# Loading and using the first two x tiles one after the other at the head of a fused state-space and feed-forward kernel

## The chip, the core and the metric

The kernel runs on one core of one Trainium2 chip. The metric is the device time of one launch in microseconds: 177.39 us before the change, the median of 3 runs (177.05 to 178.04).

## What is computed

The input x is 2048 tokens by 512 features. Both branches read its layer norm, and the output is their sum with x:

```python
x = A_x                                  # [1, 2048, 512]
xn = _layernorm(x, axis=-1)              # (x - mean) / sqrt(var + 1e-5)
# branch A: a diagonal complex state-space model, 512 states
Bu = einsum("bld,pd->blp", xn, B_bar)    # then h[t] = Lam_bar * h[t-1] + Bu[t]
y = 2.0 * einsum("blp,dp->bld", hseq, Cmat).real + xn * Dskip
# branch B: SwiGLU, w_gate and w_up [512, 1376], w_down [1376, 512]
z = (silu(xn @ w_gate) * (xn @ w_up)) @ w_down
return x + y + z
```

## The kernel before, in words

Tokens are cut into 16 tiles of 128 and four chunks of 512 (four tiles each). The 512 features are four blocks of 128 (`KD = 4`, index `k`; `HK = 2`). Most of the time is one long stream of matmuls on TensorE. In each chunk there are the projection to the states (L387), the gate and up projections (L462), the down projection (L630) and the state-space output (L643). VectorE does the rotations and scans of the state-space model beside them, and ScalarE (ACT) takes results out of PSUM.

Nothing reorders the instructions: each engine runs its own in the order in which the program emits them. From the second half of chunk 0 on, a backlog with a cost for each step (`queue`, `pump`, `need`) spreads VectorE's work between the matmuls. The head, with which the change deals, is written out by hand.

**Loads of the head (L128 to L146).** SP's queue loads x tile 0 (L128, 128 KB), then the four up rows (L133), then gate rows 0 and 1, x tile 2, gate row 2, x tile 3, gate row 3, the ends of both weights (`w_end`, L140 and L141) and x tiles 4 to 7 (L146). A row is one block `k` of 128 features by the first 1024 columns of a weight (256 KB, `load_row`, L122). Two groups of 512 columns are taken from it (`gi` 0 and 1). ACT's queue loads x tile 1 (L130), behind a small memset on VectorE (L129) that it has to wait for.

**Tiles 0 and 1 (L727 to L753).** Nine warming matmuls on constants run first (`dummy`, L703). Then the raw x tile is transposed on TensorE, block by block (`raw_mm`, L237). Meanwhile VectorE sums the rows of the tile (`sum_dve`, L229), and a small matmul subtracts the mean in PSUM (`cT_mean`, L245). Each block is then copied to SBUF by ACT (even `k`) or VectorE (odd `k`) (`raw_copy`, L252). The copies are the stationary operand of the up projection (`row_mm`, through `sw_mm`, L506). In `row_mm(0, k)`, row `k` of the up weights is multiplied for tile 0 and tile 1, with two column groups each: four matmuls of 512 columns, accumulated over `k` in four PSUM banks (`pair[0]`). The transposed blocks pass through the other four banks (`raw`): tile 0 has one bank for each block, and tile 1 has two banks with two blocks each.

**Around it.** VectorE computes the statistics of tiles 0 and 1 behind its copies (`ln_stats`, L189), GpSimd the reciprocal deviation `rstd` (L199), and VectorE the normalized tiles (`norm_dve`, L207). ACT scales the up results by `rstd` on the way out of PSUM (`sw_up`, L526). Gate row 0 follows on TensorE (`row_mm(1, 0)`), then the parameters' transpose (L278), gate rows 1 and 2, the transposes of the centered tile 2 (L237 again) and gate row 3. The normalized tiles are later transposed by SP's queue (L258), and the matrices B behind them (L150). TensorE reads those from about 23 us on (L387).

Of the kernel before, what the change touches and what calls it, by code (L numbers as in the profile page):

```python
# [23 lines left out]
def kernel(  # L24
# [17 lines left out]
    nc = tc.nc  # L42
# [9 lines left out]
    KD = D // 128  # L52
# [31 lines left out]
    x_v = A_x[0].rearrange("(n p) d -> p n d", p=128)  # L84
    out_v = out[0].rearrange("(n p) d -> p n d", p=128)
    wg_v = B_w_gate.rearrange("(k p) f -> p k f", p=128)
    wu_v = B_w_up.rearrange("(k p) f -> p k f", p=128)


    xall = const.tile([128, NT, D], BF16, name="xall")  # L90
# [5 lines left out]
    wu01 = const.tile([128, KD, FE], BF16, name="wu01")  # L96
# [24 lines left out]
    def load_row(q, t, view, k):  # L121
        q.dma_start(out=t[:, k, :], in_=view[:, k, 0:FE])  # L122

    HK = KD // 2
# [1 line left out]
    make_identity(nc, ident[:])  # L126
    minus_mean = const.tile([128, 128], BF16, name="minus_mean")
    nc.sync.dma_start(out=xall[:, 0, :], in_=x_v[:, 0, :])  # L128
    nc.vector.memset(xall[:, 1, 0:2], 0.0)  # L129
    nc.scalar.dma_start(out=xall[:, 1, :], in_=x_v[:, 1, :])  # L130
    nc.scalar.preload_act_table_set("silu_and_others")
    for k in range(KD):
        load_row(nc.sync, wu01, wu_v, k)  # L133
    for k in range(HK):
        load_row(nc.sync, wg01, wg_v, k)
# [49 lines left out]
    def by_k(ap):  # L185
        return ap.rearrange("p (k d) -> p k d", d=128)
# [36 lines left out]
    sums = const.tile([128, 2], BF16, name="sums")  # L223
# [4 lines left out]
    def sum_dve(i, dst):  # L228
        nc.vector.scalar_tensor_tensor(out=xnT[:, NCH - 1, i, 0:HW], in0=xall[:, i, 0:HW], scalar=1.0,  # L229
                                       in1=xall[:, i, HW:D], op0=ALU.mult, op1=ALU.add, accum_out=dst)  # L230
# [3 lines left out]
    raw = [pair[0][1] + pair[1][0], pair[1][1] * 2]  # L234

    def cT_mm(ps, src, k, first, stop):
        nc.tensor.matmul(ps[:, k * 128:(k + 1) * 128], lhsT=src[:, k * 128:(k + 1) * 128], rhs=ident[:], start=first,  # L237
                         stop=stop)

    def raw_mm(i):  # L240
        for k in range(KD):
            cT_mm(raw[i][k], xall[:, i, :], k, all(p is not raw[i][k] for p in raw[i][:k]), False)

    def cT_mean(i, *ks):
        nc.tensor.matmul(by_k(raw[i][ks[0]][:])[:, ks[0]:ks[-1] + 1:HK], lhsT=sums[:, i:i + 1].to_broadcast([128, 128]),  # L245
                         rhs=minus_mean[:, None, :].to_broadcast([128, len(ks), 128]), start=False, stop=True)

    def raw_copy(i, k):
        cT_copy(V.tensor_copy if k % 2 else nc.scalar.copy, raw[i][k], i, k, k + 1)

    def cT_copy(copy, ps, i, k0=0, k1=KD):
        copy(out=xcT[:, k0:k1, i * 128:(i + 1) * 128], in_=by_k(ps[:, k0 * 128:k1 * 128]))  # L252
# [21 lines left out]
    V = nc.vector  # L274
# [228 lines left out]
    def sw_mm(ps, groups, gi, i, k0=0, k1=KD):  # L503
        a, b = fgroups[gi]
        for k in range(k0, k1):
            nc.tensor.matmul(ps[:, 0:(b - a) * 128], lhsT=tokens(i, k), rhs=groups[gi][:, k, 0:(b - a) * 128],  # L506
                             start=(k == 0), stop=(k == KD - 1))
# [219 lines left out]
    dummy(warm, 4, CW)  # L727
    dummy(warm, 5, 128)
    nc.vector.tensor_scalar(out=minus_mean[:], in0=ident[:], scalar1=-1.0 / D, scalar2=None, op0=ALU.mult)
    for i in range(2):  # L730
        sum_dve(i, sums[:, i:i + 1])
    raw_mm(0)
    for k in range(HK):
        cT_mean(0, k)
        raw_copy(0, k)
    raw_mm(1)
    for k in range(HK, KD):
        cT_mean(0, k)
    for k in range(HK):
        cT_mean(1, k, k + HK)  # L740
        raw_copy(1, k)
    for k in range(HK, KD):
        raw_copy(0, k)
    for k in range(HK, KD):
        raw_copy(1, k)

    def row_mm(which, k):
        for i in range(2):
            for gi in range(2):
                sw_mm(pair[which][i][gi], (U, G)[which], gi, i, k, k + 1)  # L750

    for k in range(KD):
        row_mm(0, k)  # L753
    for i in range(2):
        ln_stats(i)
        ln_rstd(i, i + 1)
# [3 lines left out]
    for n in range(2):  # L760
        norm_dve(n)
    row_mm(1, 0)
    pp = prm_transpose()
    ln_stats(2)
# [6 lines left out]
    for k in range(1, SW):  # L771
        row_mm(1, k)
# [172 lines left out]
```

## Time and profile before

| | us |
|---|---|
| median of 3 runs | 177.39 (177.05 to 178.04) |
| the profiled execution | 178.12 |
| its span | 176.0 |
| busy: TensorE, weight loads, VectorE, ACT, GpSimd | 171.0, 82.0, 157.4, 102.3, 27.1 |
| x tile 0 arrives, by VectorE's first sum | 3.07 |
| first matmul with an up row | 4.82 |
| first matmul with up row 1 | 6.49 |
| first matmul with gate row 0 | 9.08 |

The span runs from the first to the last recorded instruction, and the time of the launch is 2.12 us longer. In the profile's rows a group of instructions stands with its line, engine, operation, `out<-in` and count; what is in brackets is the idle time of the engine ahead of it and what ended it. PE is TensorE, PEld its weight loads, DVE VectorE, POOL GpSimd, SPq and ACTq the sequencers of SP and ACT that issue DMAs. A matmul of 512 columns is recorded with some 379 ns from start to end, but matmuls overlap, so the distance between two starts is what one costs.

### The profile page before, as it was taken

Reading aid. Unit: us, or ns where it says so; the run is one execution under the profiler, and the core shown is the slowest. Engines: PE = TensorE matmul, PEld = TensorE weight load, DVE = VectorE, ACT = ScalarE, POOL = GpSimd, SP = SyncE. Lnnn points to the kernel's source line nnn. Section 1 sums busy time; section 2 is a strip of 40 time slices with the busy share of each in tenths; the row PEclk is TensorE's granted clock in tenths of the full one; section 3 lists DMA queues with packets and bytes.
Section 4 is the critical chain, followed back from the end, with each engine's and each line's share of the span. In section 5 each row is a group of like instructions: output and inputs, shape, how many; then the busy total and the mean of one; then the engine's idle time right before and its main releaser. Section 6 shows DMA issues by size and latency. Waiting matters only on the chain.

```text
span 176.0 us, 2435 instructions
## 1 busy us (share of the span) xinstructions
PE 171.0 (97%) x878; PEld 82.0 (47%) x894; DVE 157.4 (89%) x260; ACT 102.3 (58%) x188; POOL 27.1 (15%) x36
## 2 busy tenths in 40 slices
PE   8899999999999999999999999999999999999993
PEld 5444445564444464444444444446444444444542
DVE  3767999999999999999999999999999999589642
ACT  3179589794996689976044362014666652983100
POOL 5234110022000000000302500014100000530700
PEclk9999999999999999999999999999999999999999
DMA  5998969999999300220005830006310000597741
GB/s 152 370 342 80 194 110 181 303 202 293 169 207 274 115 4 0 50 61 0 2 4 111 94 34 0 0 4 68 53 22 0 0 4 0 70 164 124 93 89 60
DMA packets 34027, 18.05 MB, mean 103 GB/s; under 512 B 24512, under 2 KB 32832, under 8 KB 33888
## 3 DMA queue, kind: packets, MB, share of 16 engines
q1 hardware_dynamic: 30272, 14.39, 35.0%
q0 software_dynamic: 3456, 3.28, 14.6%
q10 hardware_dynamic: 288, 0.23, 0.4%
q8 instruction: 7, 0.11, 0.3%
q14 instruction: 4, 0.03, 0.1%
HBM read 8.33 MB, written 5.24 MB: 77 GB/s over the span
## 4 chain that ended last, share of the span: by engine, by line
PE 94%; DMA 3%; issue 1%; SPq 0%; ACT 0%; DVE 0%; ACTq 0%
PE ps L462 29%; PE ps L630 20%; PE ps L643 16%; PE ps L387 16%; PE ps L506 7%; PE ps L555 3%; DMA wu<-in_B_w_up_dram 3%; PE ps L805 2%; PE ps L620 2%; ACT u L489 0%; SPq L122 0%; SPq L128 0%; DVE xall L646 0%; PE ps L237 0%; PE ps L278 0%
## 5 line engine op out<-in xcount | busy, mean ns | idle before, releaser
L429 DVE TENSOR_TENSOR_SCAN g<-r_t,car,u 128x512 bf16<-128x512 f32 x24 | 28.8, 1263 | 0.0
L643 PE MATMUL ps<-CF,wt 128*128 128x512 bf16 (+2 forms) x133 | 28.2, 366 | 0.2
L387 PE MATMUL ps<-xnT,BT 128*128 128x512 bf16 x125 | 28.1, 379 | 0.2
L630 PE MATMUL ps<-wd_sb,guT 128*128 128x512 bf16 (+2 forms) x129 | 26.5, 362 | 0.1
L462 PE MATMUL ps<-xnT,wu 128*128 128x512 bf16 x94 | 24.5, 379 | 0.2
L462 PE MATMUL ps<-xnT,wg 128*128 128x512 bf16 x93 | 24.3, 379 | 0.1
L389 ACT CAST u<-ps 128x512 bf16<-128x512 f32 x32 | 17.8, 591 | 5.0 <-PE ps L387 4.1
L489 ACT CAST u<-ps 128x512 bf16<-128x512 f32 x30 | 17.8, 592 | 4.8 <-PE ps L462 4.8
L643 PEld LDWEIGHTS <-wt 128*128 128x128 bf16 x136 | 12.9, 98 | 15.0 <-DVE xall L600 0.4
L387 PEld LDWEIGHTS <-BT 128*128 128x128 bf16 x128 | 12.5, 98 | 14.9 <-DMA BT<-in_A_B_re_dram 0.3
L630 PEld LDWEIGHTS <-guT 128*128 128x128 bf16 x130 | 12.4, 98 | 13.8
L199 POOL TENSOR_TENSOR rstd<-ve,neg_half 128x1 f32<-128x1 f32 (+1 forms) x7 | 7.0, 1001 | 73.0 <-DVE ve L198 72.6
L652 ACT CAST res<-ps 128x512 bf16<-128x512 f32 x12 | 6.9, 582 | 18.5 <-PE ps L643 18.5
L592 ACT ACTIVATE xr<-xall,nb,rstd 128x512 bf16<-128x512 bf16 x16 | 11.8, 804 | 8.7 <-DVE xall L600 5.0
L653 POOL DMA_DIRECT2D out_dram<-res x12 | 10.5, 1043 | 35.6 <-ACT res L652 30.0
L462 PEld LDWEIGHTS <-wu 128*128 128x128 bf16 x96 | 9.4, 98 | 11.3
L488 ACT ACTIVATE guT<-ps 128x512 bf16<-128x512 f32 x20 | 12.1, 604 | 4.0 <-PE ps L462 3.6
L462 PEld LDWEIGHTS <-wg 128*128 128x128 bf16 x96 | 9.3, 98 | 10.6
L212 ACT ACTIVATE xn<-xall,nb,rstd 128x512 bf16<-128x512 bf16 x8 | 6.3, 816 | 8.8 <-DVE nb L202 8.8
L189 DVE BATCH_NORM_STATS2 stats<-xall 128x6 f32<-128x512 bf16 x16 | 10.8, 675 | 0.6 <-DMA xall<-in_A_x_dram 0.6
L462 PE MATMUL ps<-xnT,w_end 128*128 128x512 bf16 x47 | 10.8, 379 | 0.1
L397 DVE TENSOR_TENSOR pm<-g,c 128x2048 bf16<-128x2048 bf16 x8 | 9.8, 1222 | 0.1
(132 smaller groups left out, 235.3 us busy)
## 6 DMA issues: line engine op xcount, KB each, us to landing
out_dram<-in_A_x_dram SPq DMA_DIRECT2D x8, 192.0 KB, 3.2
out_dram<-res POOLq DMA_DIRECT2D x12, 128.0 KB, 3.1
out_dram<-xall POOLq DMA_DIRECT2D x3, 512.0 KB, 6.4
wd_sb<-in_B_w_down_dram SPq DMA_DIRECT2D x1, 1280.0 KB, 7.8
wu<-in_B_w_up_dram SPq DMA_DIRECT2D x4, 256.0 KB, 4.9
wg<-in_B_w_gate_dram SPq DMA_DIRECT2D x4, 256.0 KB, 5.5
xall<-in_A_x_dram SPq DMA_DIRECT2D x1, 1024.0 KB, 7.0
xall<-in_A_x_dram SPq DMA_DIRECT2D x1, 512.0 KB, 6.1
```

Source lines behind the costliest of these rows:

```text
L189: nc.vector.bn_stats(out=stats[:, n, 0, :], in_=xall[:, n, :])
L387: nc.tensor.matmul(ps[:] if c else by_k(ps[:]), lhsT=BT[:, part, k, q * 128:(q + 1) * 128], rhs=xnT[:, c, k, :] if c else xnT0[:, k], star ...
L389: nc.scalar.copy(out=u_tiles[c][:, part, q, :], in_=ps[:])
L429: V.tensor_tensor_scan(out=g()[:, part, q, :], data0=r_t[:, q:q + 1].to_broadcast([128, CW]), data1=u_tiles[c][:, part, q, :], initial=ini ...
L462: nc.tensor.matmul(ps[:fs, lo:hi], lhsT=wslice(groups, fi, k), rhs=xnT[:, c, k, lo:hi], start=(k == 0), stop=(k == KD - 1))
L488: nc.scalar.activation(out=gu(c, fi, fi + 1)[:fs, 0, :], in_=psg[:fs], func=ACT.Silu)
L489: nc.scalar.copy(out=u_pair[c][:fs, fi % 2, :], in_=psu[:fs])
L506: nc.tensor.matmul(ps[:, 0:(b - a) * 128], lhsT=tokens(i, k), rhs=groups[gi][:, k, 0:(b - a) * 128], start=(k == 0), stop=(k == KD - 1))
L592: nc.scalar.activation(out=box["xr"][:], in_=xall[:, n, :], func=ACT.Identity, scale=rstd[:, n:n + 1], bias=nb[:, n:n + 1])
L630: nc.tensor.matmul(o_tiles[n, b][:, 0:hi - lo], lhsT=gu(c, fi, fi + 1)[:, 0, i * 128:(i + 1) * 128], rhs=wd_sb[:, fi, lo:hi], start=(fi == ...
L643: nc.tensor.matmul(o[:, 0:hi - lo], lhsT=w_tiles[c][:, part, q, i * 128:(i + 1) * 128], rhs=CF[:, part, q, lo:hi], start=False, stop=(part ...
L653: nc.gpsimd.dma_start(out=out_v[:, n, lo:hi], in_=res[:, lo:hi], accum_op=ALU.add)
```

## The change

Tile 1's load goes from ACT's queue to SP's, behind up rows 0 and 1, and the memset ahead of it goes away. Tile 0 is transposed, centered and copied completely first, and goes alone through up rows 0 and 1. Then come tile 1's transposes and means; all four of its copies are on ACT now. Tile 0's row 2 follows, then tile 1's rows 0 to 2, and row 3 for both. VectorE's sum of tile 1 stands behind its two copies of tile 0 and ahead of the statistics. The number of matmuls, transposes and copies stays the same.

```diff
     nc.sync.dma_start(out=xall[:, 0, :], in_=x_v[:, 0, :])
-    nc.vector.memset(xall[:, 1, 0:2], 0.0)
-    nc.scalar.dma_start(out=xall[:, 1, :], in_=x_v[:, 1, :])
     nc.scalar.preload_act_table_set("silu_and_others")
-    for k in range(KD):
+    for k in range(HK):
+        load_row(nc.sync, wu01, wu_v, k)
+    nc.sync.dma_start(out=xall[:, 1, :], in_=x_v[:, 1, :])
+    for k in range(HK, KD):
         load_row(nc.sync, wu01, wu_v, k)
...
     def raw_copy(i, k):
-        cT_copy(V.tensor_copy if k % 2 else nc.scalar.copy, raw[i][k], i, k, k + 1)
+        cT_copy(V.tensor_copy if k % 2 and i == 0 else nc.scalar.copy, raw[i][k], i, k, k + 1)
...
-    for i in range(2):
-        sum_dve(i, sums[:, i:i + 1])
+    def row_mm(which, k, tiles=range(2)):
+        for i in tiles:
+            for gi in range(2):
+                sw_mm(pair[which][i][gi], (U, G)[which], gi, i, k, k + 1)
+
+    sum_dve(0, sums[:, 0:1])
     raw_mm(0)
-    for k in range(HK):
+    for k in range(KD):
         cT_mean(0, k)
         raw_copy(0, k)
+    for k in range(HK):
+        row_mm(0, k, (0,))
+    sum_dve(1, sums[:, 1:2])
     raw_mm(1)
-    for k in range(HK, KD):
-        cT_mean(0, k)
     for k in range(HK):
         cT_mean(1, k, k + HK)
+    for k in range(KD):
         raw_copy(1, k)
-    for k in range(HK, KD):
-        raw_copy(0, k)
-    for k in range(HK, KD):
-        raw_copy(1, k)
-
-    def row_mm(which, k):
-        for i in range(2):
-            for gi in range(2):
-                sw_mm(pair[which][i][gi], (U, G)[which], gi, i, k, k + 1)
-
-    for k in range(KD):
-        row_mm(0, k)
+    row_mm(0, HK, (0,))
+    for k in range(HK + 1):
+        row_mm(0, k, (1,))
+    row_mm(0, KD - 1)
     for i in range(2):
         ln_stats(i)
```

## The prediction, made before the run

> **What bounds the kernel now.** I read the page first (engine totals, chain), then busy time by stretches, then the head of the chain in order of time.
>
> ```profile
> span 176.0 us, 2435 instructions
> PE 171.0 (97%) x878; PEld 82.0 (47%) x894; DVE 157.4 (89%) x260; ACT 102.3 (58%) x188; POOL 27.1 (15%) x36
> PE 94%; DMA 3%; issue 1%; SPq 0%; ACT 0%; DVE 0%; ACTq 0%
> ```
>
> TensorE is busy for 97% of the span and is 94% of the chain that ended last. The 3% of DMA is what a change of the load order can touch. By stretches (span, then busy time of PE, PEld, DVE, ACT, POOL, then clock, DMA share, GB/s):
>
> ```profile
> 0.00:3.00 3.00, 2.22 (x9) 1.05 (x9) 0.32 (x4) 1.28 (x1) 2.08 (x9) 1.00 0.35 111
> 3.00:6.50 3.50, 2.90 (x21) 1.92 (x20) 2.54 (x10) 0.87 (x4) 0.54 (x2) 1.00 0.98 302
> 6.50:13.00 6.50, 6.45 (x33) 3.04 (x34) 4.61 (x17) 3.27 (x6) 2.79 (x5) 1.00 1.07 364
> 23.00:150.00 127.00, 126.37 (x646) 60.15 (x660) 124.74 (x179) 78.87 (x146) 10.88 (x12) 1.00 0.40 81
> ```
>
> From 6.50 on TensorE is full (6.45 of 6.50, later 126.37 of 127), so whatever time the head ends later or earlier passes to the end of the kernel. The DMA engines are full from 3.00 to 13.00 (shares 0.98 and 1.07), so a load of these first microseconds lands when the bytes ahead of it have moved, not when it was issued. The chain in order of time shows the wait that counts:
>
> ```profile
> 1.20 0.41 SPq L122
> ...
> 1.65 4.80 DMA wu<-in_B_w_up_dram
> 6.45 0.04 issue
> 6.49 3.61 PE ps L506 x16
> ```
>
> TensorE's last real wait is for up row 1, issued at 1.65 and landed at 6.45. From 6.49 sixteen matmuls run without a gap: the 12 of rows 1 to 3 (two tiles, two column groups each) and the 4 of gate row 0. The timeline shows the main instructions before and after it (start, duration, idle time before in brackets):
>
> ```profile
> 3.09 0.61 PE L237 MATMUL ps<-ident,xall 128*128 128x128 bf16 x4
> 3.56 0.39 PE L245 MATMUL ps<-minus_mean,sums 128*128 128x128 bf16 x2
> ...
> 4.82 1.07 PE L506 MATMUL ps<-wu,CF 128*128 128x512 bf16 x4
> 6.49 2.75 PE L506 MATMUL ps<-wu,CF 128*128 128x512 bf16 x12 [0.60 <-DMA wu<-in_B_w_up_dram]
> 9.08 1.03 PE L506 MATMUL ps<-wg,CF 128*128 128x512 bf16 x4
> ```
>
> Twelve matmuls start from 6.49 to 9.08, so one costs (9.08 - 6.49) / 12 = 0.216 us. 9.08, the start of gate row 0, is the time I recompute.
>
> **When the loads land.** The landing times of x tiles 0 and 1, of row 0 alone, and SP's issues of later loads:
>
> ```profile
> 0.74 0.40 SPq L128 DMA_DIRECT2D xall<-in_A_x_dram  x1
> 0.90 0.37 ACTq L130 DMA_DIRECT2D xall<-in_A_x_dram  x1
> 1.20 1.83 SPq L122 DMA_DIRECT2D wu<-in_B_w_up_dram  x4
> DMA to landing us min/median/max: 2.3/2.4/2.5
> DMA to landing us min/median/max: 2.9/2.9/2.9
> 6.47 0.33 SPq L122 DMA_DIRECT2D wg<-in_B_w_gate_dram  x1
> 7.12 0.39 SPq L118 DMA_DIRECT2D w_end<-in_B_w_gate_dram  x1
> 7.80 0.37 SPq L118 DMA_DIRECT2D w_end<-in_B_w_up_dram  x1
> SPq L118 <- DMA wu<-in_B_w_up_dram: 0.6, 2, 0.3
> ```
>
> The first landing row is that of the two x tiles: tile 0 at 0.74 + 2.3 = 3.04, tile 1 at 0.90 + 2.5 = 3.40. The second is row 0: 1.20 + 2.9 = 4.1. The issues at 7.12 and 7.80 each waited for an up row (last line: two waits), so rows 2 and 3 landed then. That is 0.68 us for a row of 256 KB, thus 0.34 for a 128 KB x tile.
>
> **The change part by part.**
>
> *The load of tile 1 moves* from ACT's queue to SP's, behind rows 0 and 1. Row 3 and all later SP issues come one issue later (1.83 / 4 = 0.46 us). That costs nothing while the DMA engines are backed up: row 2 was issued near 2.1 and landed at 7.12. The bytes up to and including tile 1 are now those that before went up to and including row 1. So tile 1 lands where row 1 did, at **6.45**, 3 us later than before; row 1 lands 0.34 earlier, at 6.11; rows 2 and 3 stay at 7.12 and 7.80. Tile 0 may land up to 0.3 earlier without tile 1 beside it, and row 0 by 0.34; both are worth nothing, since the wait for row 1 follows. The memset L129 and the ACT issue that go were on no waited path.
>
> *What tile 1 needs after landing.* Tile 0's own chain is the price list:
>
> ```profile
> 3.07 0.42 DVE L229 SCALAR_TENSOR_TENSOR xnT<-xall 128x256 bf16<-128x256 bf16 x1 [1.53 <-DMA xall<-in_A_x_dram]
> 3.42 0.08 DVE L229 DVE_READ_ACCUMULATOR xnT<-xall 128x1 bf16 x1
> 3.89 0.27 ACT L252 CAST CF<-ps 128x128 bf16<-128x128 f32 x1 [1.30 <-PE ps L245]
> 4.85 0.60 ACT L252 CAST CF<-ps 128x128 bf16<-128x128 f32 x3 [0.69 <-PE ps L245]
> ```
>
> From the landing at 3.04: sum to 3.50, mean matmul at 3.56 (+0.52), first copy 3.89 to 4.16 (+1.12). With about 0.08 until the matmul that reads it, tile 1's first row matmul can start 1.2 after landing: 6.45 + 1.2 = 7.65. Its four copies are now all on ACT. Three take 0.60, so one follows the other in about 0.17, while TensorE uses one per two matmuls (0.43): the copies stay ahead.
>
> *TensorE, step by step.* Tile 0's transposes, means and row 0 (2 matmuls) are over by 5.0, even if those two take 0.43 each. It waits for row 1: 6.11 + 0.04 = 6.15. Row 1 of tile 0, 2 x 0.216: 6.58. Tile 1's transposes, landed meanwhile, four at full speed 0.22 (row below): 6.80. Mean: not before 6.45 + 0.52 = 6.97; two of 256 columns, 0.22: 7.19. Row 2 of tile 0 (landed 7.12): 7.62. Tile 1's rows 0 to 2 from 7.65, 6 matmuls, then row 3, 4 matmuls: 10 x 0.216 = 2.16, to **9.81**. Against 9.08 that is **+0.73 us**. The number of matmuls is the same. Before, only one wait stood ahead of the last 12; now tile 1's transposes, means and copies stand behind 6.45 too, and only 4 of those 12 matmuls can fill the time until 7.65.
>
> ```profile
> 11.89 0.22 PE ps L237 x4
> ...
> 7.84 0.66 POOL L199 TENSOR_TENSOR rstd<-ve,neg_half 128x1 f32<-128x1 f32 x1 [0.42 <-DVE ve L198]
> 8.54 0.41 DVE L207 TENSOR_SCALAR CF<-xall,mv,rstd 128x512 bf16<-128x512 bf16 x1 [0.46 <-POOL rstd L199]
> 8.70 2.42 ACT L526 ACTIVATE u<-ps,rstd 128x512 bf16<-128x512 f32 x4 [3.25 <-PE ps L506]
> 9.55 0.69 DVE L189 BATCH_NORM_STATS2 stats<-xall 128x6 f32<-128x512 bf16 x1 [0.60 <-DMA xall<-in_A_x_dram]
> 5.67 0.68 DVE L189 BATCH_NORM_STATS2 stats<-xall 128x6 f32<-128x512 bf16 x1
> 23.10 0.82 PEld L387 LDWEIGHTS <-BT 128*128 128x128 bf16 x5 [0.26 <-DMA BT<-in_A_B_re_dram]
> ```
>
> *The wait added on VectorE.* The sum of tile 1 waits until 6.45, and behind it on that engine are the statistics of tile 0 (at 5.67 before). They now start at about 6.95, 1.28 later. Normalizing tile 1 ends near 8.95 + 1.28 = 10.2. Statistics of tile 2 then start at 10.2 rather than 9.55 (they used to wait 0.60 for their load), so VectorE is 0.65 late, less than TensorE's 0.73. The scaled copies on ACT (8.70) move with TensorE to 9.4; tile 1's rstd, 1.28 after 7.84 + 0.66 = 8.5, is there at 9.8, before ACT's second one at 10.0. What is late next is SP's transposes behind tile 3's normalization and the B matrices behind these; TensorE waits 0.26 for them at 23.10. Moved by 0.65 against TensorE's 0.73, that wait doesn't grow. If this cover fails, it costs at most a further 0.7.
>
> **Bounds.** The time of row 1 is the uncertain term. After row 0 it took 6.45 - 4.1 = 2.35 us, where later rows take 0.68. The rate (GB/s) in 40 slices of the first 9 us shows a trough:
>
> ```profile
> GB/s 0 0 0 0 0 0 0 14 32 250 337 373 346 369 437 301 55 127 209 248 275 355 312 312 391 356 373 374 384 347 401 402 414 410 364 401 423 387 378 401
> ```
>
> It falls to 55 at 3.6 us. If the trough is usually smaller, row 1 before may land at 5.5 and TensorE runs on from 5.89: 5.89 + 12 x 0.216 = 8.48. After: tile 1 at 5.5, its matmuls from 6.7, 8.86: +0.38. The profiled execution took 178.12, 0.73 more than the median 177.39, so typical ones may be nearer to this. I take +0.7, the row that is there, for 178.1, with +0.4 to +1.0 for the size alone.
>
> **The clock.** In the head a 512-column matmul takes twice its later time. Two weight loads of the warming matmuls, one matmul apart:
>
> ```profile
> 1.16 0.15 PEld L703 LDWEIGHTS <-const-bfloat16-1.0 128*128 128x128 bf16 x1 [0.28 <-issue]
> 1.59 0.15 PEld L703 LDWEIGHTS <-const-bfloat16-1.0 128*128 128x128 bf16 x1 [0.28 <-issue]
> ```
>
> They are 0.43 us apart, and the matmuls at 4.82 are the first at 0.216, though the granted clock reads 1.00 throughout. The change puts a TensorE gap from about 5.0 to 6.15 where there was one of 0.60. If the faster rate comes only after it, the matmuls behind pay 0.21 more each. [...]
>
> **The rivals.**
> 1. *The trough belongs to two queues at once.* It comes right after tile 1's load on ACT's queue. With one queue it may go: row 1 at 4.44, tile 1 at 4.78, its matmuls at 6.3, 8.5 in place of 9.08: -0.6, 176.8. Against: both x tiles had landed at 3.40, before it.
> 2. *The slow rate lasts past the gap*: if its rise takes again the 4 us that it took from TensorE's start at 0.75 to 4.82, some 8 matmuls from 6.15 on are slow: 8 x 0.21 = +1.7 on the forecast, 179.8. It decides when the rate has not risen by 5.0. Against: the warming matmuls still keep TensorE busy until then.
> 3. *The lateness grows downstream*: VectorE, 124.74 of 127 us busy, or the B transposes end later than TensorE: 0.7 more, 178.8.
> 4. *It is hidden anyway*: row 1 usually lands early and a later wait takes up the rest, 177.4.
>
> **How the numbers follow.** Forecast 0.55 (0.17 of it above +0.89 us), rival 1 0.12, rival 2 0.08, rival 3 0.12, rival 4 0.13. A measurement of this kernel can tell about 0.5%, 0.89 us, from no change: bounds 176.50 and 178.28. Slower: 0.17 + 0.08 + 0.12 = 0.37. Faster: half of rival 1, with scatter, 0.07. Within: 0.56. Range 176.9 to 179.0: it leaves out rival 2 and most of the time below rival 1.
>
> **What would show it.** Right: the sum of tile 1 on VectorE starts near 6.45 behind a DMA wait; TensorE waits for row 1 near 6.1; gate row 0 starts near 9.8; the shift at 23 and at the end is the same. Wrong: tile 1 lands before 5.5 (rival 1), matmuls 0.43 apart after 6 us (rival 2), a wait for B over 0.5 us (rival 3), gate row 0 at 9.1 or sooner.

## The result and the profile after

The changed kernel takes **178.32 us**, the median of 15 runs (177.84 to 178.67), beside 177.53 us (177.05 to 178.43) for the kernel before on the same chip. The ratio is **1.0038**, with a 95% interval of 1.0026 to 1.0050: 0.67 us slower, where +0.7 was forecast. (The two medians differ by 0.79.) The profiled execution took 178.67 us. A run more than 1.5% above the fastest of its kernel is left out of every ratio here; there is one, of 181.96 us, of the kernel called order back below.

The page of the changed kernel has nearly the same totals. The chain's DMA share is 2% in place of 3%:

```profile
span 176.5 us, 2432 instructions
PE 171.4 (97%) x878; PEld 81.8 (46%) x894; DVE 156.8 (89%) x257; ACT 103.0 (58%) x190; POOL 27.2 (15%) x36
PE 94%; DMA 2%; SPq 1%; issue 1%; DVE 0%; ACT 0%; ACTq 0%
```

Lines after the edited place differ from those of before by one or a few (L230 is now `sum_dve`, L238 the transposes, L246 the means, L507 the projections). Part of the head of the chain in order of time (start, duration, what) shows what took the place of row 1:

```profile
2.12 4.17 DMA xall<-in_A_x_dram
6.29 0.02 issue
6.31 0.45 DVE xnT L230 x2
6.76 0.05 issue
6.80 0.39 PE ps L246 x2
7.20 3.45 PE ps L507 x16
```

The chain now waits for tile 1, issued at 2.12 and landed at 6.29. Its sum on VectorE and its means on TensorE follow on the chain, and only then sixteen matmuls without a gap. Before, the sixteen stood directly behind a DMA that landed at 6.45. The timeline of the same execution:

```profile
4.64 1.60 PE L507 MATMUL ps<-wu,CF 128*128 128x512 bf16 x4 [0.61 <-DMA wu<-in_B_w_up_dram]
6.31 0.43 DVE L230 SCALAR_TENSOR_TENSOR xnT<-xall 128x256 bf16<-128x256 bf16 x1 [1.95 <-DMA xall<-in_A_x_dram]
6.33 0.40 PE L238 MATMUL ps<-ident,xall 128*128 128x128 bf16 x4
7.03 2.75 PE L507 MATMUL ps<-wu,CF 128*128 128x512 bf16 x12
9.62 1.03 PE L507 MATMUL ps<-wg,CF 128*128 128x512 bf16 x4
9.86 0.69 DVE L190 BATCH_NORM_STATS2 stats<-xall 128x6 f32<-128x512 bf16 x1
173.85 0.29 DVE L647 TENSOR_TENSOR xall<-ps,jidx 128x128 bf16<-128x128 f32 x1 [0.25 <-PE ps L644]
```

Gate row 0 starts at 9.62, where it was 9.08: +0.54. The last instruction on VectorE starts at 173.85. In the trace of before it is this one:

```profile
173.31 0.29 DVE L646 TENSOR_TENSOR xall<-ps,jidx 128x128 bf16<-128x128 f32 x1 [0.25 <-PE ps L643]
```

The difference is again 0.54. In these two traces what the head lost reached the end whole: 173.31 - 9.08 = 164.23 and 173.85 - 9.62 = 164.23.

### The profile page after: what moved, and what is told of

The parts are those of the page before. It is cut to its first block, busy times and chain, and to the rows that moved or that the text cites. A ratio compares the mean times of both kernels' runs of the same rounds, so it can differ in the third digit from the quotient of the medians.

```text
span 176.5 us, 2432 instructions
## 1 busy us (share of the span) xinstructions
PE 171.4 (97%) x878; PEld 81.8 (46%) x894; DVE 156.8 (89%) x257; ACT 103.0 (58%) x190; POOL 27.2 (15%) x36
## 4 chain that ended last, share of the span: by engine, by line
PE 94%; DMA 2%; SPq 1%; issue 1%; DVE 0%; ACT 0%; ACTq 0%
PE ps L463 29%; PE ps L631 20%; PE ps L644 16%; PE ps L388 16%; PE ps L507 7%; PE ps L556 3%; DMA xall<-in_A_x_dram 2%; PE ps L804 2%; PE ps L621 2%; SPq L122 0%; ACT u L490 0%; DVE xnT L230 0%; SPq L128 0%; PE ps L246 0%; DVE xall L647 0%
```

## The experiments

Theory A says that the head ends a fixed time after whatever tile 1's transposes, sum and means have to wait for. Its rivals are that only the late load counts, that the new order or the copies on ACT count, and that VectorE ends last. Each kernel was timed beside the kernel before on the same chip (medians 177.76, 177.89 and 177.84 us, one for each group of four).

| kernel | median us | ratio to before, 95% interval | gate row 0 starts | span |
|---|---|---|---|---|
| loads back | 178.69 | 1.0063 [1.0037, 1.0089] | 11.12 | 178.0 |
| tile 1 behind row 2 | 178.66 | 1.0076 [1.0047, 1.0105] | 9.48 | 176.4 |
| copies shared again | 178.74 | 1.0049 [1.0032, 1.0066] | 9.32 | 176.8 |
| tile 1 behind row 0 | 178.32 | 1.0031 [1.0018, 1.0045] | 9.75 | 176.7 |
| order back | 180.59 | 1.0120 [1.0080, 1.0160] | 9.91 | 176.9 |
| row 1 in halves | 178.45 | 1.0033 [1.0016, 1.0050] | 8.56 | 175.9 |
| no parameter loads | 177.80 | 0.9989 [0.9972, 1.0007] | 8.88 | 175.8 |
| loads back, kept busy | 178.70 | 1.0042 [1.0025, 1.0059] | 10.20 | 177.1 |
| halves, early index row | 178.31 | 1.0029 [1.0014, 1.0043] | 8.99 | 176.4 |
| before, early index row | 177.67 | 0.9989 [0.9976, 1.0002] | 8.69 | 175.6 |
| changed, early index row | 178.21 | 1.0022 [1.0006, 1.0038] | 9.22 | 176.1 |
| copies shared, early index row | 178.21 | 1.0029 [1.0019, 1.0040] | 8.95 | 175.9 |

The last two columns are those of the one profiled execution. The span less the start of gate row 0 is 166.9 to 167.0 us in nine of these traces, and 166.92 and 166.88 before and after the change. The three others are the copies shared again (167.48) and the two with row 1 in halves (167.34 and 167.41).

### Loads back

The order of work of the changed kernel, with the loads of before:

```diff
+    nc.vector.memset(xall[:, 1, 0:2], 0.0)
+    nc.scalar.dma_start(out=xall[:, 1, :], in_=x_v[:, 1, :])
     nc.scalar.preload_act_table_set("silu_and_others")
-    for k in range(HK):
-        load_row(nc.sync, wu01, wu_v, k)
-    nc.sync.dma_start(out=xall[:, 1, :], in_=x_v[:, 1, :])
-    for k in range(HK, KD):
+    for k in range(KD):
         load_row(nc.sync, wu01, wu_v, k)
```

> The changed kernel's order of work, with the loads of before (tile 1 on ACT's queue at the start). Tile 1 lands near 3.4 us, row 1 near 6.45. Theory A (the head ends 3.33 us after whatever stands ahead of tile 1's transposes on TensorE: its late landing, or row 1's matmuls of tile 0): transposes now wait for row 1, gate row 0 starts near 10.0, 0.4 us later than in the changed kernel, time near 178.7. Rival B (only the late load of tile 1 costs): gate row 0 near 9.1, time as before, 177.5.

178.69 us. An early tile 1 doesn't help this order, so the load alone is not the cause, and rival B (177.5) is out. Eight of its eleven runs took 178.0 to 178.9. The other three took 180.1 to 180.3, and the profiled one is among these. Its chain:

```profile
5.97 0.04 issue
6.01 1.01 PE ps L506 x2
7.02 0.43 PE ps L237 x4
7.45 0.43 PE ps L245 x2
7.87 4.27 PE ps L506 x16
```

Row 1 landed at 5.97. Tile 1's transposes stand behind it, although tile 1 had long landed. The four transposes take 0.43 where they took 0.22 at 11.89 in the trace of before, so TensorE still ran at its slow rate at 7 us. That is rival 2 of the prediction, in another kernel, and the main reason why gate row 0 starts at 11.12 here and not near 10.0. The median and the interval include these three runs.

### Loads back, TensorE kept busy

The same kernel with two dummy matmuls in the wait:

```diff
-    for k in range(HK):
-        row_mm(0, k, (0,))
+    row_mm(0, 0, (0,))
+    dummy(pair[1][1][0], 2, CW)
+    row_mm(0, 1, (0,))
     sum_dve(1, sums[:, 1:2])
```

> The first experiment's kernel (loads of before, changed order of work) with two warming matmuls of 512 columns on constants in the wait for row 1. Theory (its executions near 180 us kept the slow matmul rate because TensorE idled in the wait): none of them near 180, all within 178.0 to 179.2, and the trace shows starts 0.216 us apart from 6 or 7 us on. Rival (those executions have another cause): a quarter of them near 180 again.

All seven runs lie between 178.47 and 178.95 us. The chain of the profiled one, from the same place on:

```profile
5.98 0.85 PE ps L703 x2
6.83 0.50 PE ps L506 x2
7.33 0.22 PE ps L237 x4
7.55 0.22 PE ps L245 x2
7.77 3.45 PE ps L506 x16
```

The transposes are at 0.22 again, and sixteen matmuls take 3.45 in place of 4.27. This agrees with the theory, but is a hint and no proof: at a rate of 3 in 11, seven runs without a long one come up by chance about one time in nine. No trace of a short run of the kernel without the dummies is there to compare with. In this trace the dummies may also cost time: the chain has them from 5.98 on, and row 1's matmuls stand behind them at 6.83 without a wait for their load.

### Order back

The loads of the changed kernel, with tile 1's transposes ahead of every row, as before. It is the kernel before with this edit:

```diff
-    nc.vector.memset(xall[:, 1, 0:2], 0.0)
-    nc.scalar.dma_start(out=xall[:, 1, :], in_=x_v[:, 1, :])
     nc.scalar.preload_act_table_set("silu_and_others")
-    for k in range(KD):
+    for k in range(HK):
+        load_row(nc.sync, wu01, wu_v, k)
+    nc.sync.dma_start(out=xall[:, 1, :], in_=x_v[:, 1, :])
+    for k in range(HK, KD):
         load_row(nc.sync, wu01, wu_v, k)
```

> The loads of the changed kernel (tile 1 behind rows 0 and 1) with the order of work of before (tile 1's transposes ahead of every row matmul). Theory A: tile 1 lands at 6.0 to 6.3 and all 16 row matmuls stand behind it: gate row 0 near 10.4, 0.8 us later than in the changed kernel, 179.1 in executions at the fast matmul rate; some may keep the slow rate, since TensorE has nothing to do for 2 us, and end 1.5 to 2 us later. Rival (the order of work made the loss, not the load): as before, 177.6.

Two of the six runs took 179.0 and 179.1 us, and four took 180.4 to 182.0. The timeline of the 179.0:

```profile
5.76 0.40 PE L238 MATMUL ps<-ident,xall 128*128 128x128 bf16 x4 [1.94 <-DMA xall<-in_A_x_dram]
6.46 3.62 PE L507 MATMUL ps<-wu,CF 128*128 128x512 bf16 x16
9.91 1.03 PE L507 MATMUL ps<-wg,CF 128*128 128x512 bf16 x4
```

TensorE stands still for 1.94 us, and all 16 row matmuls are still to come. Gate row 0 came at 9.91 and not at 10.4, because tile 1 landed at 5.71. From tile 1's first transpose to gate row 0 it takes 9.91 - 5.76 = 4.15, four matmuls more than the 9.62 - 6.33 = 3.29 of the changed kernel.

So the new loads alone lose more than the whole change: the ratio is 1.0120 against 1.0038, and even the two runs near 179.0 are 1.1 us above the 177.89 of before. The new order alone loses about as much as the whole change: without its three long runs loads back is about 0.5% above before, and kept busy its ratio is 1.0042 [1.0025, 1.0059] beside 1.0038 [1.0026, 1.0050]. Once tile 1's work stands behind row 1 in the order, the late load adds nothing that can be told from these times. Either half is enough for a loss, and the pair stays behind the old pair.

### Tile 1 behind row 2

```diff
-    for k in range(HK):
+    for k in range(3):
         load_row(nc.sync, wu01, wu_v, k)
     nc.sync.dma_start(out=xall[:, 1, :], in_=x_v[:, 1, :])
-    for k in range(HK, KD):
+    for k in range(3, KD):
         load_row(nc.sync, wu01, wu_v, k)
```

> The changed kernel with tile 1's load one up row later (behind rows 0 to 2). Theory A: tile 1 lands 0.68 us later, near 6.95, gate row 0 starts 0.66 us later, near 10.3, time near 179.0. Rival C (the loss is TensorE's order or the four copies on ACT, not the landing): gate row 0 at 9.6 as in the changed kernel, 178.3.

Nine of the twelve runs took 178.3 to 179.2 us, and three 180.3 to 180.6, which the interval includes; without these three the kernel is about 0.5% slower than before. The expected 0.66 isn't there in the trace: gate row 0 starts at 9.48.

```profile
6.17 0.42 DVE L230 SCALAR_TENSOR_TENSOR xnT<-xall 128x256 bf16<-128x256 bf16 x1 [1.81 <-DMA xall<-in_A_x_dram]
9.48 1.03 PE L507 MATMUL ps<-wg,CF 128*128 128x512 bf16 x4
```

The miss is in the landing, not in what follows: tile 1 came at 6.14 with one more row ahead of it. The time of landing differs from one execution to the next by as much as a row is worth, so this run's time can't separate theory A from rival C. What follows the landing is fixed: gate row 0 starts 9.48 - 6.17 = 3.31 after the sum starts, as in the changed kernel (9.62 - 6.31 = 3.31). The changed loads and order give the same figure in three more traces below.

### Copies shared again

```diff
-        cT_copy(V.tensor_copy if k % 2 and i == 0 else nc.scalar.copy, raw[i][k], i, k, k + 1)
+        cT_copy(V.tensor_copy if k % 2 else nc.scalar.copy, raw[i][k], i, k, k + 1)
```

> The changed kernel with tile 1's copies shared by ACT and VectorE again. Theory A: the copies stay ahead of TensorE either way, no change, 178.3, gate row 0 at 9.6. Rival C (four copies in a row on ACT are late): 0.2 to 0.4 us faster, 178.0.

178.74 us, not faster. The timeline:

```profile
6.01 0.42 DVE L230 SCALAR_TENSOR_TENSOR xnT<-xall 128x256 bf16<-128x256 bf16 x1 [1.62 <-DMA xall<-in_A_x_dram]
6.93 0.49 DVE L253 CAST CF<-ps 128x128 bf16<-128x128 f32 x2 [0.49 <-PE ps L246]
9.32 1.03 PE L507 MATMUL ps<-wg,CF 128*128 128x512 bf16 x4
14.77 0.69 DVE L542 TENSOR_TENSOR guT<-guT,u 128x1024 bf16<-128x1024 bf16 x1
14.78 1.54 POOL L286 TENSOR_TENSOR r_t<-e_t,dre 128x4 f32<-128x4 f32 x1 [0.28 <-DVE ws L291]
16.88 0.88 DVE L302 TENSOR_SCALAR pm<-jidx,ws 128x512 f32<-128x512 f32 x2 [1.42 <-POOL jidx L786]
174.13 0.29 DVE L647 TENSOR_TENSOR xall<-ps,jidx 128x128 bf16<-128x128 f32 x1 [0.25 <-PE ps L644]
```

The copies do stay ahead of TensorE: 9.32 - 6.01 = 3.31 again. But from gate row 0 to the last instruction it takes 174.13 - 9.32 = 164.81, 0.58 more than before. The profile's chain shows why. It leads from VectorE's sum through the statistics to GpSimd's powers and its index row `jidx`, then through VectorE's first step on the tables (L302) and along VectorE to 91.79, and to TensorE through a transposed tile:

```profile
88.15 3.55 DVE g L430 x3
91.79 2.93 ACT xn L213 x4
94.74 5.45 DMA xnT<-xn
100.24 7.08 PE ps L388 x32
```

In the changed kernel this table step stands here:

```profile
15.69 0.88 DVE L302 TENSOR_SCALAR pm<-jidx,ws 128x512 f32<-128x512 f32 x2 [0.52 <-POOL jidx L786]
```

It starts 15.69 - 9.62 = 6.07 after gate row 0 there, and 16.88 - 9.32 = 7.56 after it here. Two copies ahead of the statistics, and a power of 1.54 in place of 1.01, made it 1.49 later, and that cost 0.58. So VectorE is a second bound, in the changed kernel some 0.9 us behind TensorE; this is an estimate from the two traces. Moving the copies to ACT, which the prediction costed at nothing, kept VectorE out of the way in the trace. The measured times don't show it by themselves, since the ratios 1.0049 and 1.0038 have intervals that overlap.

### The index row at the start

`jidx` needs no input, but is made behind the powers. Four kernels make it at the start, to take VectorE's chain off. The two-chain theory in their expectations says that the span is the later of two times: 166.9 us after gate row 0 (TensorE's chain), and 159.9 us after VectorE's first table step (VectorE's chain, read from the shared copies):

```diff
     jidx = const.tile([128, CW], F32, name="jidx")
+    nc.gpsimd.iota(out=jidx[:], pattern=[[1, CW]], base=0, channel_multiplier=0,
+                   allow_small_or_imprecise_dtypes=True)
...
-    nc.gpsimd.iota(out=jidx[:], pattern=[[1, CW]], base=0, channel_multiplier=0,
-                   allow_small_or_imprecise_dtypes=True)
```

> The changed kernel with tile 1's copies shared by ACT and VectorE, and the index row made at the start. Two-chain theory: without the index row VectorE's chain is clear again and the span is 166.9 after gate row 0; about 0.4 us below the 178.7 of the shared copies, 178.3. Rival (the copies on VectorE cost it directly): 178.7.

178.21 us, 0.5 below the 178.74. These two were timed on different chips, and the intervals of their ratios overlap (1.0019 to 1.0040 and 1.0032 to 1.0066), so the trace has to decide. It is bound by TensorE again:

```profile
5.64 0.43 DVE L232 SCALAR_TENSOR_TENSOR xnT<-xall 128x256 bf16<-128x256 bf16 x1 [1.28 <-DMA xall<-in_A_x_dram]
8.95 1.03 PE L509 MATMUL ps<-wg,CF 128*128 128x512 bf16 x4
15.01 0.88 DVE L304 TENSOR_SCALAR pm<-jidx,ws 128x512 f32<-128x512 f32 x2
```

The table step no longer waits, and the span is 175.9 - 8.95 = 166.95 after gate row 0. The 3.31 holds too (8.95 - 5.64).

> The changed kernel, with the index row made at the start. Two-chain theory: its trace is bound by TensorE with VectorE 0.9 us clear, so no change, 0.3 to 0.4% above before; the span 166.9 after gate row 0. Rival (the change lost its time on VectorE's chain): as fast as before or faster.

178.21 us, ratio 1.0022 [1.0006, 1.0038]: still slower than before, and not to be told from the changed kernel's 1.0038 [1.0026, 1.0050]. In the trace the sum starts at 5.91 and gate row 0 at 9.22, 3.31 later, and the chain leads along TensorE. So the change didn't lose its time on VectorE's chain.

> The kernel before, with the index row made at the start. Two-chain theory: executions that end on VectorE's chain get faster, the others stay; 0 to 0.3 us below before, the span 166.9 after gate row 0. Rival (only TensorE's chain counts in the kernel before): no change.

177.67 us, ratio 0.9989 [0.9976, 1.0002]: not to be told from no change. The changed kernel with the same early index row took 178.21 on the same chip, 0.54 more, so the change loses about the same without that chain.

### Tile 1 behind row 0

```diff
-    for k in range(HK):
+    for k in range(1):
         load_row(nc.sync, wu01, wu_v, k)
...
-    for k in range(HK):
-        row_mm(0, k, (0,))
+    row_mm(0, 0, (0,))
     sum_dve(1, sums[:, 1:2])
...
-    row_mm(0, HK, (0,))
-    for k in range(HK + 1):
-        row_mm(0, k, (1,))
+    row_mm(0, 0, (1,))
+    row_mm(0, 1)
+    row_mm(0, 2)
```

> Tile 1's load behind row 0 alone; on TensorE tile 0's row 0, tile 1's transposes and means, tile 1's row 0, then rows 1 to 3 for both tiles. Theory A: tile 1 lands near 4.95, is usable near 6.4, and 14 matmuls of 0.216 are left: gate row 0 near 9.4 to 9.5, 0.15 us before the changed kernel, 178.1 to 178.2, not as good as before. Rival B (the landing alone counts): 1.3 us earlier than the changed kernel, until row 1's landing bounds it, so as before or better, 177.5 or less.

178.32 us, slower than before, so rival B's 177.5 is out. The time lies near theory A's 178.1 to 178.2, but not for its reason. In the profiled execution tile 1's sum starts at 4.57, and the wait is now elsewhere:

```profile
8.02 1.89 PE L507 MATMUL ps<-wu,CF 128*128 128x512 bf16 x8 [0.28 <-DMA wu<-in_B_w_up_dram]
9.75 1.03 PE L507 MATMUL ps<-wg,CF 128*128 128x512 bf16 x4
```

Row 2 landed as late as 7.98 here, so gate row 0 was late for another reason than the one expected, and the nearness of the time is luck.

### No parameter loads

The three parameter loads on GpSimd's queue are left out of the kernel before:

```diff
-    nc.gpsimd.memset(prm_rows[:], 0.0)
-    for i, v in enumerate((A_Lambda_re, A_Lambda_im, A_log_dt)):
-        nc.gpsimd.dma_start(out=prm_rows[i * NQ:(i + 1) * NQ, :], in_=v.rearrange("(q j) -> q j", j=128))
+    nc.gpsimd.memset(prm_rows[:], -0.5)
```

> The kernel before without the three small parameter loads on GpSimd's queue (the parameters are a constant -0.5, so the state-space result is another; all the work on it stays). If these loads make the trough in the transfer rate at 2.5 to 4 us: row 1 lands by 5.5, gate row 0 near 8.5, 0.5 us below before. If they do not: row 1 near 6.4, gate row 0 near 9.1, as before.

177.80 us, no change. The rate (GB/s) in 40 slices of the first 9 us still has its trough, at 200 from 3.4 us on:

```profile
GB/s 0 0 0 0 0 0 0 32 164 310 382 373 351 346 310 200 200 246 264 209 282 391 373 319 346 300 246 264 255 310 328 373 378 360 410 401 414 378 392 410
```

So these loads don't make the trough. It is shallower here than the 55 of before, but three other traces with the parameter loads (loads back, loads back kept busy, row 1 in halves) also go down only to 182 to 184 from 3.4 us on. Row 1 was there by 5.83, an estimate from its matmuls: the eight of rows 0 and 1 end at 4.68 + 2.18 = 6.86, the last takes 0.379 and the starts are 0.216 apart. In three traces with the parameter loads and the loads of before it landed at 5.97 to 6.45. TensorE gained little from it, because it then waited 0.30 for row 2, until 7.16:

```profile
7.16 1.89 PE L504 MATMUL ps<-wu,CF 128*128 128x512 bf16 x8 [0.30 <-DMA wu<-in_B_w_up_dram]
```

### Row 1 in halves

Row 1 is loaded in two halves by columns, and the matmuls of this row and of all others in the head go by column group first, then by tile:

```diff
-    for k in range(KD):
-        load_row(nc.sync, wu01, wu_v, k)
+    load_row(nc.sync, wu01, wu_v, 0)
+    for h in range(0, FE, CW):
+        nc.sync.dma_start(out=wu01[:, 1, h:h + CW], in_=wu_v[:, 1, h:h + CW])
+    for k in range(HK, KD):
+        load_row(nc.sync, wu01, wu_v, k)
...
     def row_mm(which, k):
-        for i in range(2):
-            for gi in range(2):
+        for gi in range(2):
+            for i in range(2):
```

> The kernel before, with up row 1 loaded in two halves of 512 columns and its four matmuls in the order of the column groups. Theory A (TensorE's wait for row 1 is what is left in the head): the first half lands 0.3 us sooner, gate row 0 near 8.8, time 0.2 to 0.3 us below before. Rival: row 1's second half or row 2 is waited for in its place, no change.

> The kernel with row 1 in halves, and GpSimd's index row (L787) made at the start instead of behind the two powers of the parameters. Two-chain theory (the span is the later of 166.9 us after gate row 0 starts and 159.9 us after VectorE's first table step starts, and in the traces the table step waits for that index row): the table step moves at least 0.7 us earlier, only TensorE's chain is left, the span is 166.9 after gate row 0 within 0.1, and the time falls by 0.3 to 0.6 from the 178.45 of row 1 in halves, to about 178.0. Rival (the slower result of the halves has another cause): no change, 178.4.

178.45 us, and 178.31 with the early index row: both slower than before, and the second didn't fall to 178.0. So waiting for the index row was not the cause, and the two-chain theory missed here. In the profiled execution of the halves, 177.93 and the second fastest of twelve, gate row 0 does start at 8.56, and the last instruction on VectorE follows 164.27 later, as usual. VectorE's table step started 15.94 - 8.56 = 7.38 after gate row 0, almost as late as in the shared copies, and cost only 0.04; so the 0.9 above is no sharp limit.

```profile
172.83 0.29 DVE L649 TENSOR_TENSOR xall<-ps,jidx 128x128 bf16<-128x128 f32 x1 [0.25 <-PE ps L646]
```

But from there to the end of the span it takes 175.9 - 172.83 = 3.07, against 176.0 - 173.31 = 2.69 before. With the early index row it is 3.08 (176.4 - 173.32). Both have one DMA more in all than the kernel before. The number on SP's queue alone can't be the reason, because the changed kernel has as many there, and its end takes 176.5 - 173.85 = 2.65. Why the end is longer by 0.38 was not tried and stays open, and so does why most runs of the halves are slower than the profiled one.

In the trace with the early index row the chain leads along VectorE all the same, from x tile 2, landed at 9.94, but the last instruction comes 173.32 - 8.99 = 164.33 after gate row 0, only 0.1 later than usual. No kernel here beats the one before by more than its interval.

## Why the prediction was right

**The size.** The forecast was +0.7 us; 0.38%, or 0.67 us, was measured. The profiled executions differ by 0.54 in the start of gate row 0 and in the last instruction. So the mechanism held, but a match to 0.03 is in part luck: in the traces the same sum was 0.19 too high, and it started from an execution of 178.12, 0.59 above the later median of 177.53. Its lower figure of +0.38 rests on a slip. It lets TensorE run on from 5.89, the recorded end of row 0's matmuls, where by the distance of 0.216 the next could start at 4.82 + 4 x 0.216 = 5.68. Then gate row 0 before would start at 8.28, and the figure would be +0.58.

**Tile 1's landing.** The prediction put it at 6.45, from the bytes ahead of it; it was 6.29, and the sum started at 6.31. In the other traces with the same loads the sum started at 6.01, 5.74, 5.91 and 5.64, so 6.45 was on the late side. It was on the late side for row 1 before as well: with the loads of before row 1 landed at 6.07 and 5.97 in two other traces. So both figures of the sum were high, and only their difference counts. The trough, on which the size hung, was there without tile 1's load on ACT's queue too:

```profile
GB/s 0 0 0 0 0 0 0 27 114 332 228 82 200 346 373 282 419 352 238 220 257 338 306 187 242 297 352 338 373 364 338 273 337 373 392 319 355 391 405 378
```

It came at 2.5 us and went down to 82, while tile 0 was still arriving. So it doesn't need ACT's queue, and rival 1, which had tile 1 at 4.78, is out. GpSimd's queue still had its parameter loads beside SP's here; no run leaves SP's queue alone. The landing of row 1, 6.11 in the prediction, was 1.65 + 3.6 = 5.25 by the longest landing time of the first two rows:

```profile
DMA to landing us min/median/max: 3.4/3.5/3.6
```

That was off by 0.86 and cost nothing, because tile 1 stood behind it. So the bytes ahead of tile 1 gave its landing well, but not the split: from row 1 to tile 1 it took 6.29 - 5.25 = 1.04 us, where the prediction had 0.34. The wait for row 1 near 6.1, one of its signs of being right, is not in the trace; TensorE waited 0.61 for row 0 instead.

**The steps on TensorE.** The prediction had the means 0.52 after the landing, and 6.80 - 6.29 = 0.51 was measured. Row 2 of tile 0 was expected to start at 7.19 and started at 7.03, the 0.16 of the landing earlier. The small wait until 7.65 for the first copy was not there. Gate row 0 at 9.62 against 9.81 is thus the landing's 0.16 and this wait's 0.03.

**VectorE and ACT.** Tile 2's statistics start at 9.86, 0.31 later than before, where the prediction had 10.2. TensorE's wait for the B matrices, 0.26 before, has gone. Rival 3 did not come true in the changed kernel. The trace of the shared copies puts the margin at some 0.9 us, and shows that the four copies on ACT helped to keep it. The prediction gave them no such value.

**The clock.** The first four row matmuls in the changed kernel take 1.60 us (at 4.64, above), against 1.07 for the four at 4.82 before, so TensorE was slow longer. It cost nothing, as all four lie ahead of tile 1's arrival, and the transposes at 6.33 are fast, as the forecast's sum had them: their four weight loads take 0.23 us, where those of tile 0 at 2.87 took 0.47. None of the changed kernel's 15 runs is 1.5 us above the others, as rival 2 would have it. Of the kernels with the loads back, tile 1 behind row 2 and order back, 3 of 11, 3 of 12 and 4 of 6 runs are, and one trace, that of the loads back, shows the slow rate in them. The three of tile 1 behind row 2 may have another cause: the TensorE clock that the profile gives as granted reads 0.988 to 0.990 as a mean over these runs, where every other run here has 0.997 or more, and 1.2% of 178 us is about the 2 us that they are longer by. No trace of them was kept. In the loads-back trace TensorE's waits ahead of 7 us were short (0.25 and 0.62 us by its timeline, the last over at 6.01), and the rate was still slow behind them: 0.43 for the four transposes at 7.02, and 4.27 for the sixteen matmuls from 7.87, 0.82 more than the 3.45 of the kernel kept busy. By an estimate from these numbers the first four of the sixteen were slow (0.82 / 0.216 = 3.8). What decides the rate, no run here shows.

**Whole to the end.** TensorE was full from 6.5 on before the change (6.45 of 6.50 us busy, and 126.37 of 127 from 23 to 150), so the prediction passed on the head's loss whole. The 164.23 us after gate row 0 in both traces are what it said.

## What to carry to other kernels

Where a head is bound by transfers, ask of each load how much work stands behind it: a weight row releases its matmuls at once (row 1 before landed at 6.45, and its first matmul started at 6.49), but an input that must be summed, corrected and copied first holds up all of that (tile 1 in the changed kernel landed at 6.29, its means started at 6.80 and its copies at 7.12), so it should come early. The order of work must also let it start early: in the loads-back kernel the early tile 1 gained nothing. Where one engine is full from there on, compare two heads by the start of the first instruction after them: the span followed it within 0.1 us in nine of twelve kernels. And when an edit frees one engine, look at the second chain: here VectorE was some 0.9 us behind, by the estimate from the shared copies.

## What was not expected of the hardware

**Loads in the first microseconds land differently from run to run.** With the same loads ahead, tile 1's sum started between 5.64 and 6.31 in five traces, and in another at 6.17 with a whole row more ahead. The trough in the transfer rate is there with and without the parameter loads, and with and without tile 1's load on ACT's queue; no run leaves out both. Its place goes with that load: from 2.48 to 2.70 us the rate is 82 to 191 GB/s in five traces with tile 1 on SP's queue (the changed kernel, behind row 2, copies shared, behind row 0, order back), and 346 to 387 in five with it on ACT's (before, loads back, kept busy, halves, no parameter loads), which go down to between 55 and 200 from 3.4 to 4.5 us. Its cause stays open.

**A power on GpSimd takes 1.54 us instead of 1.01** when VectorE's product of two tiles starts just ahead of it (14.77 against 14.78 in the shared copies). In the changed kernel the product starts 0.36 after the power:

```profile
14.12 1.01 POOL L286 TENSOR_TENSOR r_t<-e_t,dre 128x4 f32<-128x4 f32 x1 [0.28 <-DVE ws L291]
14.48 0.69 DVE L542 TENSOR_TENSOR guT<-guT,u 128x1024 bf16<-128x1024 bf16 x1 [0.29 <-ACT guT L515]
```

The long power takes 0.53 us more. Four traces have it (the shared copies, tile 1 behind row 0, row 1 in halves and no parameter loads), all with the product 0.01 or 0.02 us ahead of it. Where it starts 0.04 us after the power (order back), the power takes 1.01 again. Why the order of the two starts counts was not shown.
